# Gated mix of sliding attention and a Mish MLP on one core: another list of steps and other PSUM groups

## The chip, the core and the metric

The kernel runs on one core of a Trainium2 chip. The metric is the time of one execution on the device in microseconds. The core has a matmul engine (TensorE, PE in the profile), a vector engine (VectorE, DVE), a scalar engine (ScalarE, ACT), GpSimd (POOL) and SyncE (SP), which here does little but issue DMAs. Each engine runs its own instructions strictly in the order in which they were written for it, and waits on semaphores for the others.

## What is computed

With x of 2048 rows by 640 columns, all in fp32:

```python
x = A_x
g = _sigmoid((x * gate_w).sum(-1, keepdims=True))
a = _A_ref(x, A_wqkv, A_wo)     # 32 heads of 20; each row attends to itself and to the rows 2, 4 .. 14 before it
b = _B_ref(x, B_w1, B_b1, B_w2) # (mish(x @ w1 + b1)) @ w2, with 1728 hidden columns
return g * a + (1 - g) * b
```

Branch a is x @ wqkv, the windowed softmax attention, and a product with wo. Mish is h * tanh(softplus(h)).

## The kernel before

**Products.** TensorE multiplies in a reduced fp32 form, so every operand is kept as a high and a low part in one buffer (`pair`): ACT copies the rounded high part (L448), and VectorE or GpSimd subtract it to get the low part (L451). Each product is then three matmuls, high by high, high by low, low by high (L516, L517, L518), all into the same PSUM bank. To save matmuls, several products use a fast 2x2 block scheme: sums of blocks are formed on VectorE and GpSimd (L1023, L1245), products of the sums are made, and intermediate results are carried from one PSUM bank into another as a seed: ACT copies the bank (L1150) or VectorE adds to it (L832), and the next products accumulate on top.

**Stages.** Up to about 390 us the kernel works on three things interleaved. First the *units*: eight pieces of x @ wqkv (two halves of the rows by four groups of eight heads), each in eight *slots* of 128 rows. A slot is 15 matmuls of 496 columns into one bank, which ACT empties in three or four copies into the buffer `kvq` (L686, L688, L690). When all eight slots of a unit are there, SP copies the rows that neighbouring positions need within `kvq` (the halo copies, kvq from kvq, of 112 and 15 partitions), and VectorE runs the attention of that unit with multiply and reduce instructions of 2560 elements (L573, L576, L619, L623); ACT adds the exponentials (L596, with a table load) and the weighting (L600), and a copy of q (L579). Units 2 and 3 are made together with the fast scheme, in four *pairs* of slots with steps a1 to c3: a1 to a3 and b1, b2 give unit 2, and store two intermediate results in DRAM (`pu`, `pv`). c0 loads them back in one buffer with two DMAs on SP (L877); c1 copies `pu` from it into a bank (L885, ACT), called ga, and puts six matmuls on top; VectorE then makes the seed of a second bank, de, from ga and `pv` (L832); c2 and c3 finish both for unit 3.

Second the *quads*: x @ w1 in two halves of the rows and six blocks of hidden columns. A quad has banks al, be, ga, de and ep, and steps first (makes al, copied to seed be), second (makes ep, copied by ACT to an `hb` buffer, L1150), m1 to m4, l1 and l2 (the rest). Results leave a bank through Mish on ACT (L1156), or through a sum with the ep copy on VectorE (L1168) and then Mish. Each lands in one of eight `hb` buffers, from which SP stores it to DRAM (L481, the targets are `act11`, `act22`, `actt1` and the like). Sums of two results are formed in the same buffers by GpSimd or VectorE. Some of these sums are made by GpSimd's accumulating DMAs (L1533, L934). The last block of hidden columns (`last`, four banks l0 to l3) is done plainly and leaves through L946.

Third, loads and preparations: `x`, `wq`, `wa`, `wc`, `pieces`, `forms`, `sum` steps bring in inputs and form their sums.

Then the product with w2 and the product with wo follow, up to the end at 615 us. They are not part of the list of steps.

**What sets the order.** The text `ORDER` lists the steps, and at the end of the program each is executed:

```python
for token in ORDER.split():
    do(token)
```

A step only registers tasks with a planner (`class Plan`): the engine, an estimated duration, a rank, what must be done before, which buffers are taken and held. The planner then plays the program through with its estimates. Whenever an engine is free in this play, it gets, of the tasks that are ready and whose buffers are free, the one of the lowest rank and, among these, the one that was registered first; GpSimd also goes by how soon TensorE needs the result. The order that comes out is written down for each engine and is fixed on the chip. TensorE's order so follows the list only where banks and operands are there; buffers of one kind are handed out strictly in the order of the list. Another list, or another group for a bank, can therefore change the order on all five engines, also far from the entry that differs.

**PSUM banks.** Six banks are shared in two groups of three, `qb` and `sb`. A step that needs a bank names it and takes the next free one of a group; the dictionary `BANKS` overrides the group that the code gives:

```python
def bank_buf(name, ring):

    return sb_buf() if BANKS.get(name, ring) == "s" else qb_buf()
```

The name is made of the step: `u65` is unit 6 slot 5, `q12de` is bank de of quad 2 in the second half of the rows, `p22ga` is bank ga of pair 2 of units 2 and 3, `l2` a bank of the last block. A step that takes a bank waits until whoever held that bank before has been read out, and TensorE waits with it.

Of the kernel before, what the change touches and what calls it, by code (L numbers as in the profile page):

```python
# [254 lines left out]
ORDER = """
u.0.5 u.0.6 u.0.4 u.0.7 q.0.0.first last.0 wq.1 q.0.0.m1 q.0.0.m4 q.0.0.m2 sum q.0.0.second q.0.0.m3 pieces.0.1 u.1.0 last.1 u.1.2 q.0.0.l2
q.0.1.first u.1.3 q.0.0.l1 u.1.6 q.0.1.m1 q.0.1.m2 pieces.0.2 q.0.1.m4 u.1.1 q.0.1.second q.0.1.l2 sum q.0.2.first u.1.7 u.1.4 q.0.1.m3 q.0.2.m1
q.0.1.l1 u.1.5 wa.2 q.0.2.second pieces.0.3 pieces.0.4 q.0.2.m3 p.2.0.a1 q.0.2.m4 x.3.1 q.0.2.m2 q.0.2.l2 p.2.2.a1 p.2.1.a1 x.2.4 p.2.0.a2 p.2.1.a2
p.2.0.a3 q.0.2.l1 p.2.2.a2 p.2.3.a1 p.2.3.a2 x.3.3 q.0.3.first p.2.0.b2 p.2.3.a3 p.2.2.a3 p.2.0.c0 p.2.1.a3 p.2.2.b1 q.0.3.m1 p.2.0.b1 x.2.1
q.0.3.second q.0.3.m4 p.2.1.b1 p.2.2.b2 pieces.0.5 p.2.1.c0 q.0.3.m3 x.2.2 wc.2 q.0.4.first q.0.3.m2 q.0.3.l2 q.0.5.first q.0.3.l1 p.2.3.b1 q.0.4.m1  # L260
p.2.2.c0 q.0.4.second q.0.4.m2 q.0.4.m4 p.2.1.b2 p.2.3.c0 p.2.3.b2 q.0.4.m3 wq.4 q.0.4.l1 q.0.4.l2 q.0.5.m1 p.2.0.c1 p.2.2.c1 p.2.3.c1 q.0.5.m2
p.2.2.c2 x.2.3 q.0.5.m4 x.2.0 q.0.5.l2 q.0.5.second p.2.3.c2 p.2.0.c3 p.2.2.c3 p.2.3.c3 p.2.1.c1 p.2.1.c3 p.2.1.c2 x.3.2 third x.3.0 x.3.4 q.0.5.m3
p.2.0.c2 u.4.3 q.0.5.l1 u.4.1 u.4.5 rest.0 u.4.2 sum pieces.1.0 forms.1.0 u.4.7 u.4.6 q.1.0.first u.4.0 q.1.0.m1 wq.5 u.5.4 rest.1 pieces.1.1 u.5.2
u.4.4 q.1.1.first q.1.0.second sum q.1.0.m4 u.5.1 q.1.0.m3 u.5.3 sum q.1.1.second q.1.1.m2 sum u.5.6 q.1.1.m1 pieces.1.2 u.5.0 u.5.7 q.1.1.m4 wq.6
q.1.0.m2 u.5.5 q.1.2.first sum q.1.0.l2 u.6.2 u.6.4 q.1.1.l2 q.1.0.l1 q.1.2.m1 q.1.1.m3 u.6.3 wq.7 u.6.1 q.1.1.l1 u.6.5 u.6.0 u.7.2 u.6.7 u.7.3 u.7.6
q.1.2.second q.1.2.m4 sum pieces.1.3 pieces.1.4 u.6.6 sum q.1.2.m2 q.1.4.first q.1.2.m3 q.1.2.l2 u.7.5 u.7.1 q.1.3.first q.1.3.m2 u.7.4 u.7.0
q.1.3.second pieces.1.5 q.1.2.l1 q.1.3.m1 u.7.7 q.1.4.m1 q.1.4.m4 q.1.4.m2 q.1.3.m4 q.1.3.m3 q.1.3.l2 q.1.4.second q.1.3.l1 q.1.4.l2 rest.2
q.1.5.first q.1.4.m3 q.1.5.m1 q.1.4.l1 q.1.5.m4 q.1.5.m2 lastw.1 q.1.5.second q.1.5.m3 q.1.5.l1 q.1.5.l2 last.2 last.3 rest.3
"""


# [1697 lines left out]
```

## Time and profile before

| what | value |
|---|---|
| median of 3 runs | 616.08 us (615.9 to 616.94) |
| the profiled execution, its own time | 616.89 us |
| its span | 615.1 us |
| TensorE busy | 608.4 us, 99%, 2698 matmuls |
| VectorE busy | 580.3 us, 94% |
| ACT busy | 386.4 us, 63% |
| GpSimd busy | 352.4 us, 57% |
| moved by DMA | 147.01 MB, mean 239 GB/s |

The span lies within the execution; 1.8 us lie around it. The row of a timeline gives the start in us, the duration in us, the engine, the line, the operation and its buffers, and in brackets the idle time ahead of it and what ended it. A row of the stretches gives the bounds, the length, and the busy time and count of TensorE, weight loads, VectorE, ACT and GpSimd, then the granted clock, the share of the DMA engines and GB/s. A row of a DMA view gives the queue, the count, the size and the median time in us from issue to landing. In the group of a line, the numbers behind the bar are total busy us and mean ns of one instruction.

### The profile page before, as it was taken

The page shows a single profiled execution, that of the slowest core. Times are in us where ns is not written, and L with a number is a line of the kernel's source. Part 1 is how long each engine was busy: PE and PEld are TensorE (multiplying, and loading weights), DVE is VectorE, ACT ScalarE, POOL GpSimd, SP SyncE. Part 2 cuts the span into 40 slices and gives each one's busy share as a digit, 9 for nine tenths or more (in the row PEclk, how much of TensorE's full clock was granted, in tenths as well). Part 3 has the DMA queues.
Part 4 walks back from the last instruction along what each step waited for, and adds up shares of the span by engine and source line. Part 5 has one row for each costly group of instructions (what it writes and reads, how often), then busy time and mean ns, then how long its engine had stood idle before and what let it go on. Part 6 is the DMA issues. An engine that isn't in the chain of part 4 may idle for free.

```text
span 615.1 us, 9163 instructions
## 1 busy us (share of the span) xinstructions
PE 608.4 (99%) x2698; PEld 504.7 (82%) x2698; DVE 580.3 (94%) x517; ACT 386.4 (63%) x886; POOL 352.4 (57%) x334
## 2 busy tenths in 40 slices
PE   9999999999999999999999999999999999999997
PEld 6888888887878888888888887888888888888886
DVE  8899999999899999999999999999999999989955
ACT  7687747666786486745746775776857543736520
POOL 1676868967687786376564577775467963001000
PEclk9999999999999999999999999999999999999999
DMA  9774876668696867999984699998989874989913
GB/s 324 233 237 130 274 257 178 237 191 280 214 323 216 270 202 208 266 272 327 242 227 158 179 326 290 278 264 251 268 275 281 248 204 133 286 253 303 278 58 119
DMA packets 101347, 147.01 MB, mean 239 GB/s; under 512 B 11617, under 2 KB 54625, under 8 KB 101073
## 3 DMA queue, kind: packets, MB, share of 16 engines
q1 hardware_dynamic: 97936, 140.66, 70.9%
q0 software_dynamic: 3072, 5.51, 6.5%
q8 instruction: 21, 0.34, 0.2%
q10 hardware_dynamic: 288, 0.26, 0.1%
q14 instruction: 30, 0.24, 0.1%
HBM read 92.38 MB, written 53.03 MB: 236 GB/s over the span
## 4 chain that ended last, share of the span: by engine, by line
PE 93%; DMA 3%; DVE 1%; POOL 1%; issue 1%; ACT 0%; SPq 0%; DVEq 0%; POOLq 0%; ACTq 0%
PE qb L516 15%; PE qb L518 15%; PE qb L517 15%; PE sb L516 15%; PE sb L518 15%; PE sb L517 15%; DMA raw<-in_wq 1%; DMA pair<-pu 1%; DMA actt<-hb 1%; PE qb L680 1%; DVE pr L573 0%; POOL pair L451 0%; DVE lg L576 0%; POOL raw L1023 0%; PE sb L523 0%
## 5 line engine op out<-in xcount | busy, mean ns | idle before, releaser
L451 POOL TENSOR_TENSOR pair<-raw,pair 128x512 fp32r<-128x512 f32 (+3 forms) x142 | 178.0, 1282 | 84.5 <-ACT pair L448 48.2
L448 ACT ACTIVATE pair<-raw 128x512 fp32r<-128x512 f32 (+3 forms) x235 | 136.1, 611 | 49.6 <-PE sb L518 15.8
L516 PE MATMUL qb<-pair 128*128 128x512 f32 (+1 forms) x387 | 150.1, 388 | 2.0 <-ACT qb L885 1.3
L518 PE MATMUL qb<-pair 128*128 128x512 f32 (+1 forms) x387 | 150.0, 388 | 0.0
L517 PE MATMUL qb<-pair 128*128 128x512 f32 (+1 forms) x387 | 149.9, 387 | 0.0
L516 PE MATMUL sb<-pair 128*128 128x512 f32 (+2 forms) x384 | 148.4, 386 | 0.1
L518 PE MATMUL sb<-pair 128*128 128x512 f32 (+2 forms) x384 | 148.2, 386 | 0.0
L517 PE MATMUL sb<-pair 128*128 128x512 f32 (+2 forms) x384 | 148.2, 386 | 0.0
L573 DVE TENSOR_TENSOR pr<-kvq,qg 128x2560 f32<-128x2560 f32 x32 | 90.0, 2811 | 2.6 <-ACT qg L579 1.4
L619 DVE TENSOR_TENSOR pr<-kvq,pg 128x2560 f32<-128x2560 f32 x32 | 90.2, 2820 | 1.0
L576 DVE TENSOR_REDUCE lg<-pr 128x128 f32<-128x2560 f32 x32 | 90.1, 2816 | 0.7
L623 DVE TENSOR_REDUCE kvq<-pr 128x320 f32<-128x2560 f32 x32 | 90.1, 2815 | 0.6
L516 PEld LDWEIGHTS qb<-pair 128*128 128x128 f32 x387 | 72.6, 188 | 17.1 <-ACT qb L885 1.7
L518 PEld LDWEIGHTS qb<-pair 128*128 128x128 f32 x387 | 72.6, 188 | 14.5
L517 PEld LDWEIGHTS qb<-pair 128*128 128x128 f32 x387 | 72.6, 188 | 14.4
L516 PEld LDWEIGHTS sb<-pair 128*128 128x128 f32 x384 | 72.1, 188 | 14.9 <-DVE sb L832 0.5
L517 PEld LDWEIGHTS sb<-pair 128*128 128x128 f32 x384 | 72.1, 188 | 14.2
L518 PEld LDWEIGHTS sb<-pair 128*128 128x128 f32 x384 | 72.1, 188 | 14.2
L451 DVE TENSOR_TENSOR pair<-raw,pair 128x512 fp32r<-128x512 f32 (+2 forms) x93 | 63.6, 705 | 2.8 <-ACT pair L448 2.4
L1023 POOL TENSOR_TENSOR raw<-raw 128x128 f32<-128x128 f32 (+3 forms) x58 | 45.4, 796 | 24.2 <-DMA raw<-in_w 11.6
L1023 POOL TENSOR_TENSOR hb<-hb 128x512 f32<-128x512 f32 x39 | 50.3, 1299 | 9.0 <-DVE lg L595 2.6
L448 ACT ACTIVATE pair<-hb 128x512 fp32r<-128x512 f32 (+3 forms) x62 | 36.5, 589 | 3.9 <-PE qb L518 2.4
(168 smaller groups left out, 745.9 us busy)
## 6 DMA issues: line engine op xcount, KB each, us to landing
actt<-hb SPq DMA_DIRECT2D x52, 256.0 KB, 3.6
raw<-in_w SPq DMA_DIRECT2D x40, 256.0 KB, 3.5
act<-hb SPq DMA_DIRECT2D x38, 256.0 KB, 4.1
raw<-actt SPq DMA_DIRECT2D x37, 256.0 KB, 3.1
raw<-in_wq SPq DMA_DIRECT2D x36, 248.0 KB, 4.1
raw<-act SPq DMA_DIRECT2D x29, 256.0 KB, 3.6
raw<-in_x SPq DMA_DIRECT2D x27, 256.0 KB, 3.7
o<-ot SPq DMA_DIRECT2D x64, 80.0 KB, 3.2
```

The costliest lines, as they stand in the source:

```text
L448: a = add("ACT", act_ns(n), lambda: A.activation(hi(), raw(), AF.Copy), after, rank=rank, take=take, hold=hold)
L451: return (V if e == "DVE" else G).tensor_tensor(lo(), raw(), hi().bitcast(F32), op=OP.subtract)
L516: nc.tensor.matmul(ps, ah, bh, start=first, stop=False, skip_group_check=more)
L517: nc.tensor.matmul(ps, ah, bl, start=False, stop=False, skip_group_check=more)
L518: nc.tensor.matmul(ps, al, bh, start=False, stop=last, skip_group_check=more)
L573: return V.tensor_tensor(pr, window(kv, s0, 0), qg[:, :, None, :].to_broadcast([128, 2, W, QF]), op=OP.mult)
L576: V.tensor_reduce(lg_w[:, s0:s0 + 2], pr.rearrange("p s w (h d) -> p s w h d", d=DH), op=OP.add, axis=AX.X)
L619: V.tensor_tensor(pairs.rearrange("p s k i (h d) -> p s k i h d", d=DH), vw, pg[:, s0:s0 + 2].rearrange("p s (k i) h -> p s k i h", i=2)[: ...
L623: V.tensor_reduce(q[:, s0:s0 + 2], pairs.rearrange("p s k i f -> p s f k i"), op=OP.add, axis=AX.XY)
L680: nc.tensor.matmul(ps.t[:, :n], X[0, kc].t[:, a, i * 128:(i + 1) * 128], WQ[0, kc].t[:, b, :n], start=a == b and kc == 0, stop=False)
L1023: return (V if e == "DVE" else G).tensor_tensor(t.t[:, i:i + n], a.t[:, j:j + n], b.t[:, k:k + n], op=op)
```

## The change

Only `ORDER` and `BANKS` differ. The steps listed are the same ones, each as often as before, and so are the operations (the rows between the `...` of the two lists are of the same kind); their order in the list, the group of many banks, and with these the instruction orders of all five engines differ.

```diff
--- before.py
+++ after.py
@@ -251,21 +251,21 @@
...
-BANKS = {'l0': 's', 'p20al': 's', 'p20de': 's', 'p20ga': 'q', 'p21de': 's', 'p22ga': 'q', 'p23ga': 'q', 'q00al': 's', 'q00be': 'q', 'q00ga': 'q', 'q02al': 's', 'q02de': 'q', 'q03be': 'q', 'q03de': 'q', 'q03ep': 's', 'q03ga': 'q', 'q04al': 's', 'q05be': 'q', 'q05ep': 's', 'q10de': 'q', 'q11al': 's', 'q11de': 'q', 'q11ga': 'q', 'q12al': 's', 'q12de': 'q', 'q13be': 'q', 'q13ga': 'q', 'q14al': 's', 'q14de': 'q', 'q14ep': 's', 'q14ga': 'q', 'q15al': 's', 'q15de': 'q', 'q15ga': 'q', 'u04': 's', 'u06': 's', 'u11': 's', 'u12': 's', 'u13': 's', 'u16': 's', 'u17': 's', 'u42': 's', 'u43': 's', 'u46': 's', 'u52': 's', 'u53': 's', 'u54': 's', 'u57': 's', 'u64': 's', 'u65': 's', 'u72': 's', 'u73': 's', 'u74': 's', 'u75': 's', 'u76': 's'}
+BANKS = {'l0': 's', 'l1': 's', 'l2': 's', 'l3': 's', 'p20al': 's', 'p20de': 's', 'p20ep': 's', 'p20ga': 'q', 'p21de': 's', 'p22ep': 's', 'p22ga': 'q', 'p23ga': 'q', 'q00ga': 'q', 'q01de': 'q', 'q01ep': 's', 'q02de': 'q', 'q02ga': 'q', 'q03ep': 's', 'q04al': 's', 'q05be': 'q', 'q05ep': 's', 'q10de': 'q', 'q12al': 's', 'q12de': 'q', 'q12ga': 'q', 'q13be': 'q', 'q13ep': 's', 'q13ga': 'q', 'q14al': 's', 'q14de': 'q', 'q14ep': 's', 'q14ga': 'q', 'q15al': 's', 'q15be': 'q', 'q15de': 'q', 'q15ep': 's', 'q15ga': 'q', 'u05': 's', 'u10': 's', 'u15': 's', 'u17': 's', 'u41': 's', 'u43': 's', 'u44': 's', 'u45': 's', 'u51': 's', 'u52': 's', 'u54': 's', 'u56': 's', 'u61': 's', 'u63': 's', 'u70': 's', 'u71': 's', 'u72': 's', 'u73': 's', 'u75': 's', 'u76': 's', 'u77': 's'}
 ORDER = """
...
-p.2.2.c0 q.0.4.second q.0.4.m2 q.0.4.m4 p.2.1.b2 p.2.3.c0 p.2.3.b2 q.0.4.m3 wq.4 q.0.4.l1 q.0.4.l2 q.0.5.m1 p.2.0.c1 p.2.2.c1 p.2.3.c1 q.0.5.m2
-p.2.2.c2 x.2.3 q.0.5.m4 x.2.0 q.0.5.l2 q.0.5.second p.2.3.c2 p.2.0.c3 p.2.2.c3 p.2.3.c3 p.2.1.c1 p.2.1.c3 p.2.1.c2 x.3.2 third x.3.0 x.3.4 q.0.5.m3
-p.2.0.c2 u.4.3 q.0.5.l1 u.4.1 u.4.5 rest.0 u.4.2 sum pieces.1.0 forms.1.0 u.4.7 u.4.6 q.1.0.first u.4.0 q.1.0.m1 wq.5 u.5.4 rest.1 pieces.1.1 u.5.2
...
-q.1.0.m2 u.5.5 q.1.2.first sum q.1.0.l2 u.6.2 u.6.4 q.1.1.l2 q.1.0.l1 q.1.2.m1 q.1.1.m3 u.6.3 wq.7 u.6.1 q.1.1.l1 u.6.5 u.6.0 u.7.2 u.6.7 u.7.3 u.7.6
-q.1.2.second q.1.2.m4 sum pieces.1.3 pieces.1.4 u.6.6 sum q.1.2.m2 q.1.4.first q.1.2.m3 q.1.2.l2 u.7.5 u.7.1 q.1.3.first q.1.3.m2 u.7.4 u.7.0
...
-q.1.5.first q.1.4.m3 q.1.5.m1 q.1.4.l1 q.1.5.m4 q.1.5.m2 lastw.1 q.1.5.second q.1.5.m3 q.1.5.l1 q.1.5.l2 last.2 last.3 rest.3
...
+q.0.5.m1 p.2.3.b1 q.0.4.m3 q.0.4.m4 x.2.1 p.2.0.c1 p.2.0.c3 p.2.2.b2 x.3.4 q.0.4.l1 p.2.3.c0 p.2.2.c1 q.0.4.l2 p.2.3.c1 q.0.5.m2 q.0.5.m4 q.0.5.l2
+p.2.2.c2 p.2.1.b2 p.2.2.c3 q.0.5.second p.2.0.c2 p.2.1.c1 p.2.3.c3 x.2.2 x.3.0 p.2.3.c2 p.2.1.c2 x.2.0 wq.4 p.2.1.c3 third u.4.5 q.0.5.m3 rest.0
...
+q.1.1.second u.5.7 u.6.1 u.5.5 u.6.6 u.6.0 q.1.1.m3 wq.7 u.6.3 u.7.6 q.1.1.l2 q.1.2.m1 u.6.7 q.1.2.second u.6.5 pieces.1.3 q.1.2.m2 u.7.3 sum u.7.0
+q.1.2.m4 pieces.1.4 u.7.1 q.1.2.m3 q.1.1.l1 u.6.4 u.6.2 q.1.3.first q.1.2.l2 q.1.3.m1 u.7.2 q.1.3.second q.1.2.l1 q.1.4.first u.7.4 pieces.1.5 sum
+q.1.3.m4 q.1.3.m3 q.1.3.l1 q.1.4.m2 q.1.4.m1 q.1.3.m2 u.7.7 u.7.5 q.1.4.m4 q.1.3.l2 q.1.4.second q.1.5.first q.1.4.m3 q.1.5.m1 q.1.4.l1 lastw.1
+q.1.5.m4 q.1.4.l2 q.1.5.second q.1.5.m2 q.1.5.m3 q.1.5.l1 q.1.5.l2 last.2 last.3 rest.2 rest.3
...
```

Three places show what that does to the queues. In the rows, `qb`, `sb`, `hb`, `pair` and `raw` are followed by a running number that tells one use of a buffer from another; "out <- in" as in the profile.

ACT around the first c1 steps of the tail of units 2 and 3 (176 us in the profile); `pair_1972`, `pair_1823` and `pair_1782` are the buffers loaded by c0. Before:

```order
L1156 ACT_TABLE_LOAD
L1156 ACTIVATE hb_2037<-qb_1765,bias_75 128x512
L885 ACTIVATE qb_2040<-pair_1972 128x496
L1156 ACTIVATE hb_2048<-sb_2001,bias_75 128x512
L1150 ACTIVATE hb_2058<-sb_2028 128x512
L885 ACTIVATE sb_2061<-pair_1823 128x496
```

And now:

```order
L1156 ACT_TABLE_LOAD
L1156 ACTIVATE hb_2037<-qb_1734,bias_75 128x512
L885 ACTIVATE qb_2040<-pair_1782 128x496
L1156 ACTIVATE hb_2047<-sb_1995,bias_75 128x512
L1150 ACTIVATE hb_2058<-sb_2029 128x512
L885 ACTIVATE sb_2061<-pair_1972 128x496
```

The first of the two seeds reads another buffer. In SP's queue the load of `pair_1972` stands at the same row before and now, and that of `pair_1782` 25 rows ahead of it; these rows are from SP's queue now:

```order
L877 DMA pair_1782<-pu2_2_260 128x496
L877 DMA pair_1782<-pv2_2_256 128x496
...
L481 DMA raw_1952<-in_wq 128x512
L481 DMA act21_0_4_101<-hb_1941 128x512
L481 DMA o1_189<-ot_1904 32x5x128
L481 DMA raw_1969<-in_wq 128x512
L877 DMA pair_1972<-pu2_1_259 128x496
L877 DMA pair_1972<-pv2_1_255 128x496
```

ACT around the copy of quad 15's ep (374 us in the profile), which frees that bank; the last row reads the bank l2 of the last block. Before:

```order
L1156 ACT_TABLE_LOAD
L1156 ACTIVATE hb_3996<-sb_3796,bias_75 128x512
L1150 ACTIVATE hb_3998<-qb_3921 128x512
L448 ACTIVATE pair_4024<-raw_3880 128x512
L1156 ACTIVATE hb_4028<-qb_3909,bias_75 128x512
...
L946 ACTIVATE hb_4076<-qb_4006,bias_75 128x512
```

And now:

```order
L1150 ACTIVATE hb_3966<-sb_3892 128x512
...
L448 ACTIVATE pair_3993<-raw_3873 128x512
L1156 ACT_TABLE_LOAD
L1156 ACTIVATE hb_3997<-sb_3821,bias_75 128x512
L448 ACTIVATE pair_4021<-raw_3878 128x512
L1156 ACTIVATE hb_4025<-qb_3922,bias_75 128x512
...
L946 ACTIVATE hb_4071<-sb_4000,bias_75 128x512
```

The copy (the L1150 row) moved from behind the table load and one Mish to six rows ahead of the table load, and ep and l2 are now in the sb group.

ACT and SP near 302 us, in the order now. `qb_3213` is the bank of unit 6 slot 5, `qb_3229` that of quad 12's de, `qb_3274` that of unit 6 slot 4; unit 6 slot 2 takes the bank of `qb_3229` next. `hb_3304` takes the buffer of `hb_3242`. ACT:

```order
L448 ACTIVATE pair_3234<-raw_3172 128x496
L1156 ACTIVATE hb_3240<-hb_3240,bias_75 128x512
L686 ACTIVATE kvq1_269<-qb_3213 128x320
L688 ACTIVATE kvq1_269<-qb_3213 128x160
L690 ACTIVATE hx_81<-qb_3213 128x16
L448 ACTIVATE pair_3268<-raw_3204 128x496
L579 ACTIVATE qg_273<-kvq0_268 128x320
L1156 ACTIVATE hb_3304<-qb_3229,bias_75 128x512
L686 ACTIVATE kvq1_269<-qb_3274 128x320
```

SP:

```order
L481 DMA raw_3244<-in_w1 128x512
L481 DMA raw_3260<-in_w1 128x512
L481 DMA raw_3264<-in_w1 128x128
L481 DMA kvq1_269<-kvq1_269 112x960
L481 DMA kvq1_269<-kvq1_269 15x960
L481 DMA actt1_1_1_133<-hb_3242 128x512
L481 DMA actt3_1_1_161<-hb_2886 128x512
```

Before, the store to `actt1_1_1_133` stands 19 rows behind the last halo copy in SP's queue; the rows around it there are:

```order
L481 DMA raw_3129<-in_wo 128x2x256
L481 DMA raw_3131<-in_wo 128x2x256
L481 DMA act22_1_1_119<-hb_2761 128x512
L481 DMA actt1_1_1_133<-hb_3123 128x512
L481 DMA actt3_1_1_161<-hb_3096 128x512
```

Now the store follows the two halo copies directly, and these wait for the L686 row of `qb_3213`.

More of the change, by code (lines that the diff above doesn't have):

```diff
@@ L255 @@
 ORDER = """
[L256 to L259, printed above, removed]
@@ L260 @@
-q.0.3.second q.0.3.m4 p.2.1.b1 p.2.2.b2 pieces.0.5 p.2.1.c0 q.0.3.m3 x.2.2 wc.2 q.0.4.first q.0.3.m2 q.0.3.l2 q.0.5.first q.0.3.l1 p.2.3.b1 q.0.4.m1
-p.2.2.c0 q.0.4.second q.0.4.m2 q.0.4.m4 p.2.1.b2 p.2.3.c0 p.2.3.b2 q.0.4.m3 wq.4 q.0.4.l1 q.0.4.l2 q.0.5.m1 p.2.0.c1 p.2.2.c1 p.2.3.c1 q.0.5.m2
-p.2.2.c2 x.2.3 q.0.5.m4 x.2.0 q.0.5.l2 q.0.5.second p.2.3.c2 p.2.0.c3 p.2.2.c3 p.2.3.c3 p.2.1.c1 p.2.1.c3 p.2.1.c2 x.3.2 third x.3.0 x.3.4 q.0.5.m3
-p.2.0.c2 u.4.3 q.0.5.l1 u.4.1 u.4.5 rest.0 u.4.2 sum pieces.1.0 forms.1.0 u.4.7 u.4.6 q.1.0.first u.4.0 q.1.0.m1 wq.5 u.5.4 rest.1 pieces.1.1 u.5.2
@@ L264 @@
-u.4.4 q.1.1.first q.1.0.second sum q.1.0.m4 u.5.1 q.1.0.m3 u.5.3 sum q.1.1.second q.1.1.m2 sum u.5.6 q.1.1.m1 pieces.1.2 u.5.0 u.5.7 q.1.1.m4 wq.6
-q.1.0.m2 u.5.5 q.1.2.first sum q.1.0.l2 u.6.2 u.6.4 q.1.1.l2 q.1.0.l1 q.1.2.m1 q.1.1.m3 u.6.3 wq.7 u.6.1 q.1.1.l1 u.6.5 u.6.0 u.7.2 u.6.7 u.7.3 u.7.6
-q.1.2.second q.1.2.m4 sum pieces.1.3 pieces.1.4 u.6.6 sum q.1.2.m2 q.1.4.first q.1.2.m3 q.1.2.l2 u.7.5 u.7.1 q.1.3.first q.1.3.m2 u.7.4 u.7.0
-q.1.3.second pieces.1.5 q.1.2.l1 q.1.3.m1 u.7.7 q.1.4.m1 q.1.4.m4 q.1.4.m2 q.1.3.m4 q.1.3.m3 q.1.3.l2 q.1.4.second q.1.3.l1 q.1.4.l2 rest.2
@@ L268 @@
-q.1.5.first q.1.4.m3 q.1.5.m1 q.1.4.l1 q.1.5.m4 q.1.5.m2 lastw.1 q.1.5.second q.1.5.m3 q.1.5.l1 q.1.5.l2 last.2 last.3 rest.3
+u.0.5 u.0.7 u.0.4 wq.1 u.0.6 q.0.0.first q.0.0.second q.0.0.m1 last.0 q.0.0.m4 q.0.0.l2 q.0.0.m3 pieces.0.1 q.0.1.first u.1.7 u.1.2 q.0.1.m1 q.0.0.l1
+q.0.1.second sum q.0.0.m2 sum q.0.1.m3 q.0.1.m4 u.1.4 pieces.0.2 u.1.3 last.1 u.1.1 q.0.1.l1 q.0.1.m2 u.1.0 q.0.1.l2 u.1.5 q.0.2.first u.1.6 wa.2
+q.0.2.m1 q.0.2.m2 q.0.2.second p.2.2.a1 p.2.1.a1 q.0.2.m4 p.2.0.a1 q.0.2.m3 p.2.0.a2 q.0.2.l1 p.2.1.a2 pieces.0.3 p.2.0.a3 q.0.2.l2 p.2.3.a1 x.2.3
@@ new lines @@
+p.2.1.a3 pieces.0.4 p.2.0.b2 p.2.1.b1 p.2.2.a2 x.2.4 x.3.2 p.2.0.b1 p.2.3.a2 p.2.3.a3 pieces.0.5 q.0.3.first q.0.3.m1 x.3.1 p.2.2.a3 p.2.2.c0 p.2.3.b2
+q.0.3.second q.0.3.m3 q.0.3.m4 q.0.3.l1 q.0.4.first q.0.4.m1 q.0.3.l2 q.0.3.m2 p.2.0.c0 q.0.4.m2 q.0.5.first x.3.3 p.2.2.b1 q.0.4.second wc.2 p.2.1.c0
+q.0.5.m1 p.2.3.b1 q.0.4.m3 q.0.4.m4 x.2.1 p.2.0.c1 p.2.0.c3 p.2.2.b2 x.3.4 q.0.4.l1 p.2.3.c0 p.2.2.c1 q.0.4.l2 p.2.3.c1 q.0.5.m2 q.0.5.m4 q.0.5.l2
+p.2.2.c2 p.2.1.b2 p.2.2.c3 q.0.5.second p.2.0.c2 p.2.1.c1 p.2.3.c3 x.2.2 x.3.0 p.2.3.c2 p.2.1.c2 x.2.0 wq.4 p.2.1.c3 third u.4.5 q.0.5.m3 rest.0
@@ new lines @@
+q.0.5.l1 pieces.1.0 sum u.4.6 u.4.7 u.4.2 forms.1.0 q.1.0.first u.4.4 u.4.0 u.4.3 wq.5 sum pieces.1.1 u.4.1 q.1.0.second q.1.0.m1 rest.1 u.5.6 u.5.2
+q.1.0.m4 u.5.3 pieces.1.2 u.5.1 q.1.1.first u.5.4 wq.6 q.1.1.m1 sum q.1.0.m3 q.1.1.m4 q.1.1.m2 sum q.1.2.first q.1.0.l2 sum q.1.0.l1 u.5.0 q.1.0.m2
+q.1.1.second u.5.7 u.6.1 u.5.5 u.6.6 u.6.0 q.1.1.m3 wq.7 u.6.3 u.7.6 q.1.1.l2 q.1.2.m1 u.6.7 q.1.2.second u.6.5 pieces.1.3 q.1.2.m2 u.7.3 sum u.7.0
+q.1.2.m4 pieces.1.4 u.7.1 q.1.2.m3 q.1.1.l1 u.6.4 u.6.2 q.1.3.first q.1.2.l2 q.1.3.m1 u.7.2 q.1.3.second q.1.2.l1 q.1.4.first u.7.4 pieces.1.5 sum
```

## The prediction

> **What bounds the kernel now.** I read the page first: part 1 for the busy shares, part 2 for the slices, part 4 for the chain that ended last.
>
> ```profile
> span 615.1 us, 9163 instructions
> PE 608.4 (99%) x2698; PEld 504.7 (82%) x2698; DVE 580.3 (94%) x517; ACT 386.4 (63%) x886; POOL 352.4 (57%) x334
> PEclk9999999999999999999999999999999999999999
> PE 93%; DMA 3%; DVE 1%; POOL 1%; issue 1%; ACT 0%; SPq 0%; DVEq 0%; POOLq 0%; ACTq 0%
> ```
>
> TensorE is busy 99% of the span, at the full granted clock in every slice, and 93% of the last chain is matmuls. The change keeps all 2698 of them, so their own time is fixed. All that a new order can win is the time in which TensorE stands still between matmuls; all that it can lose is new time of that kind. So next comes the question where TensorE stands still: the busy time in stretches of 15 us, then the rows in the stretches that are not full.
>
> ```profile
> 135.00:150.00 15.00, 14.87 (x66) 11.99 (x65) 14.66 (x9) 10.97 (x22) 10.88 (x9) 1.00 0.82 257
> 165.00:180.00 15.00, 13.64 (x59) 10.48 (x58) 14.31 (x11) 12.92 (x28) 12.01 (x11) 1.00 0.88 257
> 360.00:375.00 15.00, 14.27 (x63) 11.52 (x62) 13.49 (x14) 12.90 (x25) 12.20 (x10) 1.00 0.93 307
> 180.00:360.00 180.00, 180.00 (x808) 151.27 (x807) 176.59 (x119) 115.03 (x307) 116.04 (x122) 1.00 0.80 239
> ```
>
> The second number is TensorE's busy time. Between the start-up and 600 us only three stretches are short of their 15.00; from 180 to 360 us, for one, nothing is missing, and its 808 matmuls give the usual pace: 180 / 808 = 0.223 us from start to start, a mean of the forms of 512 columns (0.227) and 496 columns (0.220). The rows of TensorE's timeline around each stall:
>
> ```profile
> 146.64 0.39 PE L518 MATMUL qb<-kvq,pair 128*128 128x512 f32 x1
> 147.16 0.50 PE L516 MATMUL qb<-kvq,pair 128*128 128x512 f32 x1
> 147.50 0.40 PE L517 MATMUL qb<-kvq,pair 128*128 128x512 f32 x1
> ...
> 168.13 0.39 PE L518 MATMUL qb<-pair 128*128 128x512 f32 x1
> 168.63 0.49 PE L516 MATMUL sb<-pair 128*128 128x496 f32 x1
> ...
> 175.30 0.39 PE L518 MATMUL sb<-pair 128*128 128x512 f32 x1
> 176.94 0.49 PE L516 MATMUL qb<-pair 128*128 128x496 f32 x1 [1.25 <-ACT qb L885]
> ...
> 178.16 0.39 PE L518 MATMUL qb<-pair 128*128 128x496 f32 x1
> 178.51 0.49 PE L516 MATMUL sb<-pair 128*128 128x496 f32 x1
> ...
> 372.87 0.39 PE L518 MATMUL qb<-pair 128*128 128x512 f32 x1
> 373.99 0.50 PE L516 MATMUL qb<-pair 128*128 128x512 f32 x1 [0.73 <-ACT hb L1150]
> 374.32 0.39 PE L517 MATMUL qb<-pair 128*128 128x512 f32 x1
> ```
>
> The loss of a stall is the gap between the starts less the usual 0.23 or 0.22, and the first matmul behind it costs another 0.11 (its successor starts 0.33 or 0.34 later, see the rows at 147.50 and 374.32). So the stall at 147 us costs (0.52 - 0.23) + 0.11 = 0.40; the one at 168.6 us (0.50 - 0.23) + 0.11 = 0.38; the one at 177 us (1.64 - 0.23) + 0.11 = 1.52, with 0.13 + 0.11 = 0.24 more at 178.5 us, together 1.76; the one at 374 us (1.12 - 0.23) + 0.10 = 0.99. Sum 3.53 us. That is the most this order can give: with no stall left, the median 616.08 becomes 612.55.
>
> **The change part by part.** It adds and removes no instruction. For each stall I ask what TensorE waited for, and whether that comes sooner in the new order.
>
> At 177 us the first matmul of c1 (unit 2, pair 2) waits for its PSUM seed, and the seed for a transfer:
>
> ```profile
> 176.30 0.59 ACT L885 ACTIVATE qb<-pair 128x496 f32<-128x496 f32 x1 [1.89 <-DMA pair<-pu]
> 170.19 1.08 SPq L877 DMA_DIRECT2D pair<-pu  x1
> pair<-pu SPq DMA_DIRECT2D x1, 248.0 KB, 6.0
> ```
>
> The load was issued at 170.19 and took 6.0 us to land. In the new order the same place reads a pair whose load stands 25 rows earlier in SP's queue (rows 153 and 178), so it is long there: 1.52 us gone. The pair in row 178 is now read by the c1 behind it, six matmuls later (6 x 0.22 = 1.3 us). Without the stall the first c1 starts at 176.94 - 1.41 = 175.53, the second at about 176.9 at the earliest; its seed can end at 176.2 + 0.6 = 176.8 if the load is issued and lands as before. ACT's mish and a seed copy ahead of it are done by then. That is level; I take the 0.24 at 178.5 us as gone too, and carry 0.3 us for this place among the small waits below.
>
> At 374 us the last block's second output takes the qb bank of quad 15's ep, freed by a copy that stands in ACT's queue behind a table load and a mish:
>
> ```profile
> 371.47 1.28 ACT L1156 ACT_TABLE_LOAD   x1
> 372.76 0.69 ACT L1156 ACTIVATE hb<-sb,bias 128x512 f32<-128x512 f32 x1
> 373.35 0.59 ACT L1150 ACTIVATE hb<-qb 128x512 f32<-128x512 f32 x1
> ```
>
> In the new order this copy stands ahead of the table load (six rows before it), and the last block uses banks of the sb group. 0.99 us gone. At 147 us the bank of quad 05's al was freed by a mish behind others in ACT's queue; that step now comes earlier, with a bank that was freed before. 0.40 us gone. At 168.6 us the de of pair 0 waits for a late sum of VectorE, and stands at the same place of TensorE's new order: I leave that 0.38 in. So 1.52 + 0.24 + 0.99 + 0.40 = 3.15 us are taken off.
>
> Now what is late next. Going through the new order for banks that are retaken soon after their reader, one place stands out, near 302 us. Slot 2 of unit 6 takes the qb bank of quad 12's de. That bank is freed by a mish on ACT, which needs an hb buffer, which is free only when a store of the earlier hb lands; and SP issues that store right behind the two halo copies of kvq, which wait for ACT to empty the bank of unit 6's slot 5. I run a clock from the last matmul of slot 5. TensorE needs the bank after 12 matmuls of de, 15 of slot 4 and 9 of ga: 21 x 0.227 + 15 x 0.220 = 8.07 us. On the other side:
>
> ```profile
> 301.39 0.72 ACT L1156 ACTIVATE hb<-hb,bias 128x512 f32<-128x512 f32 x1 [0.61 <-DVE hb L1168]
> 304.66 0.41 ACT L686 ACTIVATE kvq<-qb 128x320 f32<-128x320 f32 x1
> 305.26 2.47 SPq L481 DMA_DIRECT2D kvq<-kvq  x2
> 82.57 0.73 ACT L1156 ACTIVATE hb<-hb,bias 128x512 f32<-128x512 f32 x1 [2.98 <-DMA act<-hb]
> ```
>
> ACT is free for the evacuation after at most one mish (0.72), and needs 0.41: 1.1 us, or 1.7 with a wait for VectorE as the 0.61 in the row. The two halo issues take up to 2.5 us; I take 1.5, since the second need not wait. The mish at the end takes 0.7, with 0.05 until TensorE goes on. The store must then land within 8.07 - (1.1 to 1.7) - 1.5 - 0.75 = 4.1 to 4.7 us. How long such a transfer takes:
>
> ```profile
> actt<-hb SPq DMA_DIRECT2D x52, 256.0 KB, 3.6
> actt<-hb SPq DMA_DIRECT2D x1, 256.0 KB, 2.0
> actt<-hb SPq DMA_DIRECT2D x1, 256.0 KB, 4.2
> ot<-o SPq DMA_DIRECT2D x1, 256.0 KB, 5.6
> ot<-o SPq DMA_DIRECT2D x1, 256.0 KB, 6.2
> ```
>
> The median of all 52 such stores is 3.6 us, the fastest (57.5 us) 2.0; one directly behind a halo copy (85 us) took 4.2; two transfers behind a halo with an accumulating DMA of GpSimd in flight (270 and 293.5 us) took 6.2 and 5.6. In the new order three loads, the halo and such a GpSimd DMA stand just ahead of the store, so the last two rows are nearest: 5.9 us, against an allowance of 4.4, is a stall of 1.5, and 0.1 for the restart: 1.6 us. Bounds: 0 (any of the first three rows), and 2.1 + 0.1 = 2.2 (6.2 against 4.1). The mish row at 82.57 us is the same wait in the old order, 2.98 us for the store of its hb; there TensorE did not stop, because no bank hung on it.
>
> [...]
>
> Last, small waits. An order planned this tight has places where a bank or a seed comes just in time; before, two of them missed by 0.40 and 0.38. One is kept already, 0.3 is the c1 above, and I add 0.3 for one more: 0.6 us, bounds 0 and 1.5 (four such misses).
>
> The sum against the median: 616.08 - 3.15 + 1.6 + 0.6 = **615.1 us**. Against the profiled execution's own 616.89 it is 615.94; that execution lies 0.81 above the median, and I keep to the median. Below 0.2% (1.23 us) a measurement of this kernel can't tell a difference from none; 615.1 is 0.95 us or 0.16% below: **no change that can be told, on the faster side**. Its own range is 614.2 to 616.6.
>
> **The rivals.**
>
> Faster: the store near 302 us lands within its allowance. The 52 stores' median of 3.6 speaks for it, the 5.6 and 6.2 behind halo and GpSimd against it. Then 615.1 - 1.6 = 613.5, and 612.55 with no small waits and the 168.6 us place clear.
>
> Slower: VectorE is one instruction late near 295 us. ACT's mish ahead of the evacuation waits for VectorE's sum L1168, and VectorE's queue holds the long attention products just ahead of it:
>
> ```profile
> L573 DVE TENSOR_TENSOR pr<-kvq,qg 128x2560 f32<-128x2560 f32 x32 | 90.0, 2811 | 2.6 <-ACT qg L579 1.4
> ```
>
> One such instruction is 2.8 us. If VectorE lags by one, evacuation, halos, store, mish and bank all move by 2.8: the stall is 1.6 + 2.8 = 4.4 us and the time 615.1 + 2.8 = 617.9. It decides from a lag of 2.2 us on (617.31, the point from which slower can be told). For it speaks that VectorE is busy 176.59 of the 180 us up to 360, so a lag isn't made up; against it that before ACT's longest wait of this kind there was 0.61. [...]
>
> Not as it says: the stall at 177 us only moves to the second c1, because the load in SP's row 178 again lands late, 1 us later than before, and near 302 us the 1.6 comes on top. Then 615.1 + 1.4 = 616.5. This is still no change.
>
> **How the numbers follow.** The main case has 0.36, the faster rival 0.33, the slower one 0.17, the moved stall 0.10; 0.04 is for gains between the cases. Of the main case a little lies under 614.85. So faster 0.38, no change 0.45, slower 0.17. The range runs from 612.7, just above the floor of 612.55, to 617.7, which leaves out most of the slower rival and little else.
>
> **What would show it.** Right: the profile of the changed kernel has TensorE's stretch from 360 to 375 us full; the seed before the first c1 near 175.5 us waits for no transfer; a stall of 1 to 2 us near 302 us, put down to ACT's L1156 on hb, and that mish itself to a DMA from hb. Wrong: no pause there (faster rival); a pause above 3 us with ACT waiting for VectorE's L1168 before it (slower rival); a pause over 1 us at a seed L885 near 177 us (moved stall); or a pause over 1 us at any place not named here, which I can't see from the order and which would make the sum wrong altogether.

## The result, and where the time went

The changed kernel takes 620.15 us (median of 9 runs, 617.22 to 621.91) against 616.24 us before (9 runs, 614.72 to 617.59). The ratio is 1.0057, with a 95% interval from 1.0041 to 1.0073, which is some 3.5 us (the medians lie 3.9 us apart): slower, clear of the 0.2% and outside the predicted range. The profiled execution took 620.64 us, with a span of 618.9 against 615.1.

The page after, parts 1 and 2:

```profile
span 618.9 us, 9169 instructions
PE 611.4 (99%) x2698; PEld 506.5 (82%) x2698; DVE 578.9 (94%) x518; ACT 387.5 (63%) x886; POOL 352.6 (57%) x333
PEclk9999999999999999999899999999999999999999
```

The busy shares in part 1 hardly differ from before. The granted clock differs in one digit: it is 8 in the slice from 294 to 309 us. The stretches of the kernel after (bounds, length, busy time and count of TensorE, weight loads, VectorE, ACT and GpSimd, then granted clock, DMA share and GB/s) show the rest:

```profile
135.00:150.00 15.00, 15.00 (x68) 12.45 (x67) 14.86 (x11) 10.66 (x23) 11.37 (x9) 1.00 0.88 254
165.00:180.00 15.00, 15.00 (x68) 12.36 (x67) 14.38 (x13) 13.84 (x32) 12.49 (x11) 1.00 1.01 321
300.00:315.00 15.00, 12.25 (x43) 9.79 (x42) 13.70 (x11) 8.40 (x21) 9.12 (x10) 0.77 0.89 236
305.00:310.00 5.00, 3.74 (x9) 3.08 (x10) 3.77 (x5) 4.03 (x12) 2.14 (x3) 0.55 0.98 327
310.00:315.00 5.00, 5.00 (x19) 4.08 (x19) 4.93 (x4) 4.38 (x9) 5.00 (x5) 0.77 0.72 151
360.00:375.00 15.00, 15.00 (x68) 12.43 (x67) 14.80 (x11) 11.84 (x26) 10.40 (x10) 1.00 0.91 299
```

The three stretches that were short before are full now. In their place the one from 300 to 315 us has 43 matmuls at a granted clock of 0.77. Before, it had 70:

```profile
300.00:315.00 15.00, 15.00 (x70) 12.72 (x69) 14.86 (x11) 10.29 (x30) 12.41 (x17) 1.00 0.90 224
```

From 310 to 315 us TensorE is "busy" all 5.00 us, but with 19 matmuls rather than the 25 of before: busy time alone doesn't show a slow clock, the count and the clock do. TensorE's timeline after, around the pause:

```profile
303.13 0.39 PE L518 MATMUL qb<-pair 128*128 128x512 f32 x1
306.26 0.78 PE L516 MATMUL qb<-pair 128*128 128x496 f32 x1 [2.75 <-ACT hb L1156]
306.84 0.61 PE L517 MATMUL qb<-pair 128*128 128x496 f32 x1
...
312.21 0.43 PE L518 MATMUL qb<-pair 128*128 128x496 f32 x1
312.48 0.39 PE L516 MATMUL sb<-pair 128*128 128x496 f32 x1
```

The pause costs 306.26 - 303.13 - 0.23 = 2.90 us. The 15 matmuls behind it take 312.48 - 306.26 = 6.22 us, some 0.41 us each, where 15 x 0.22 = 3.30 is usual: 2.92 us more. So one place costs 5.8 us, and half of it is not the wait but the clock behind it.

The account of the two spans: 3.53 us of old stalls are gone; 2.90 and 2.92 are new here; small stalls at 50 us (0.29), 65 us (0.16) and 177 us (0.15) cost 0.60; the start-up takes 0.39 more (the 101st matmul starts at 25.66 us rather than 25.27; in another execution of the same kernel it is 25.14, so this is scatter and not the change). That gives +3.3 of the +3.8 us; the other 0.5 is spread too thin for me to place.

### The profile page after: what moved, and what is told of

It is laid out like the page before. It is cut to its first block, busy times and chain, and to the rows that moved or that the text cites. A ratio compares the mean times of both kernels' runs of the same rounds, so it can differ in the third digit from the quotient of the medians.

```text
span 618.9 us, 9169 instructions
## 1 busy us (share of the span) xinstructions
PE 611.4 (99%) x2698; PEld 506.5 (82%) x2698; DVE 578.9 (94%) x518; ACT 387.5 (63%) x886; POOL 352.6 (57%) x333
## 4 chain that ended last, share of the span: by engine, by line
PE 95%; DMA 2%; ACT 1%; DVE 1%; issue 0%; SPq 0%; DVEq 0%; ACTq 0%
PE sb L516 16%; PE sb L517 16%; PE sb L518 16%; PE qb L516 15%; PE qb L517 15%; PE qb L518 15%; DMA hb<-in_x 1%; DMA kvq<-kvq 1%; DMA raw<-in_wq 1%; DVE pr L619 0%; PE qb L680 0%; ACT pair L448 0%; SPq L481 0%; PE sb L522 0%; PE qb L523 0%
## 5 line engine op out<-in xcount | busy, mean ns | idle before, releaser
L451 POOL TENSOR_TENSOR pair<-raw,pair 128x512 fp32r<-128x512 f32 (+3 forms) x136 | 170.0, 1273 | 75.9 <-ACT pair L448 60.1
L448 ACT ACTIVATE pair<-raw 128x512 fp32r<-128x512 f32 (+3 forms) x235 | 137.7, 613 | 48.8 <-DMA raw<-actt 12.8
L516 PE MATMUL sb<-pair 128*128 128x512 f32 (+2 forms) x421 | 162.7, 386 | 0.0
L517 PE MATMUL sb<-pair 128*128 128x512 f32 (+2 forms) x421 | 162.6, 386 | 0.0
L518 PE MATMUL sb<-pair 128*128 128x512 f32 (+2 forms) x421 | 162.5, 386 | 0.0
L516 PE MATMUL qb<-pair 128*128 128x512 f32 (+1 forms) x350 | 137.0, 391 | 2.7 <-ACT hb L1156 2.7
L517 PE MATMUL qb<-pair 128*128 128x512 f32 (+1 forms) x350 | 136.8, 391 | 0.0
L518 PE MATMUL qb<-pair 128*128 128x512 f32 (+1 forms) x350 | 136.6, 390 | 0.0
L516 PEld LDWEIGHTS sb<-pair 128*128 128x128 f32 x421 | 79.1, 188 | 16.1 <-ACT sb L885 0.3
L518 PEld LDWEIGHTS sb<-pair 128*128 128x128 f32 x421 | 79.0, 188 | 15.6
L517 PEld LDWEIGHTS sb<-pair 128*128 128x128 f32 x421 | 79.1, 188 | 15.5
L619 DVE TENSOR_TENSOR pr<-kvq,pg 128x2560 f32<-128x2560 f32 x32 | 90.3, 2820 | 1.0
L516 PEld LDWEIGHTS qb<-pair 128*128 128x128 f32 x350 | 66.4, 190 | 16.6 <-ACT hb L1156 3.2
L518 PEld LDWEIGHTS qb<-pair 128*128 128x128 f32 x350 | 66.4, 190 | 13.4
L517 PEld LDWEIGHTS qb<-pair 128*128 128x128 f32 x350 | 66.4, 190 | 13.2
L451 DVE TENSOR_TENSOR pair<-raw,pair 128x512 fp32r<-128x512 f32 (+3 forms) x99 | 69.4, 722 | 5.7 <-ACT pair L448 5.5
L1023 POOL TENSOR_TENSOR hb<-hb 128x512 f32<-128x512 f32 x42 | 55.2, 1331 | 11.6 <-DVE pg L609 4.0
L1023 POOL TENSOR_TENSOR raw<-raw 128x128 f32<-128x128 f32 (+3 forms) x53 | 42.5, 818 | 21.9 <-DVE raw L1023 8.4
L451 POOL TENSOR_TENSOR pair<-hb,pair 128x512 fp32r<-128x512 f32 (+2 forms) x29 | 35.0, 1211 | 15.7 <-ACT pair L448 8.1
```

Source lines behind the costliest of these rows:

```text
L448: a = add("ACT", act_ns(n), lambda: A.activation(hi(), raw(), AF.Copy), after, rank=rank, take=take, hold=hold)
L451: return (V if e == "DVE" else G).tensor_tensor(lo(), raw(), hi().bitcast(F32), op=OP.subtract)
L516: nc.tensor.matmul(ps, ah, bh, start=first, stop=False, skip_group_check=more)
L517: nc.tensor.matmul(ps, ah, bl, start=False, stop=False, skip_group_check=more)
L518: nc.tensor.matmul(ps, al, bh, start=False, stop=last, skip_group_check=more)
L619: V.tensor_tensor(pairs.rearrange("p s k i (h d) -> p s k i h d", d=DH), vw, pg[:, s0:s0 + 2].rearrange("p s (k i) h -> p s k i h", i=2)[: ...
```

## The experiments

Three theories and a question. **Pause and clock**: the store of one hb buffer lands late, TensorE stops for 2.9 us, and the stop itself lowers the clock. **Rival A**: the clock falls by itself in this order. **Rival B**: the store is late because the DMA engines are full, wherever it stands in its queue. The question within the first: what makes that store's landing so long: the halo copies ahead of it, or GpSimd's accumulating DMA.

For the edits a few tasks got a name, and a task can be held back: the planner plays as before, but the held instruction is written out only behind another one that is named. So all other rows of all five engines stay in place.

```diff
+HOLD, held = {}, []
+def emit(t, e):
+    ins = held.append((HOLD[t.tag], t.fn)) if t.tag in HOLD else t.fn(e) if t.both else t.fn()
+    return [x[1]() for x in held if x[0] == t.tag and t.tag] and None or ins
...
-                    ins = t.fn(e) if t.both else t.fn()
+                    ins = emit(t, e)
...
```

**The store three rows sooner.** One load and the two halo copies are held until the store.

```diff
-HOLD, held = {}, []
+HOLD, held = {x: ("put", "t1", 1, 1) for x in (("dc", 3), ("halo", 6, 0, 0), ("halo", 6, 0, 1))}, []
```

> The changed kernel with one edit on SyncE's queue: near 297 us the store of the hb buffer is issued ahead of one small load and of the two halo copies, three rows sooner. Theory (the pause of 2.9 us near 303 us comes from the late store, and the half clock behind it from the pause): the store is issued 1.5 to 2 us sooner, the pause shrinks to about 1 us, the granted clock is 1.000 and the time falls by 1.8 + 3.0 to about 615.3 us. Rival A (the clock falls by itself in this order, not through the pause): the time falls by 1.8 us only, to 618.3, with the clock still 0.994 to 0.997. Rival B (the store is late because the DMA engines are full, wherever it stands): the pause stays at 2.9 us and the time at 620.

Measured: 614.30 us (10 runs, 613.59 to 615.91) against 616.91 before on the same chip (25 runs); ratio 0.9956, interval 0.9936 to 0.9976. Its stretch from 300 us, and then, of its timeline, the store's issue and the mish that waits for the landing:

```profile
300.00:315.00 15.00, 15.00 (x70) 12.74 (x69) 14.90 (x11) 9.52 (x27) 10.96 (x13) 1.00 0.91 251
```

```profile
295.56 0.33 SPq L481 DMA_DIRECT2D actt<-hb  x1
...
299.07 0.69 ACT L1156 ACTIVATE hb<-qb,bias 128x512 f32<-128x512 f32 x1 [1.11 <-DMA actt<-hb]
```

The store was issued at 295.56 and the mish that waits for it began at 299.07: 3.5 us. No pause is left and the clock is 1.00. Rivals A and B both fall. The gain was larger than expected, since the landing shrank too. This kernel is 2.6 us faster than the one before and 5.1 to 5.9 us faster than the one after (619.39 and 620.15), from three rows of SP's queue.

**Useless work in the pause.** Zero weights times ones, added to the bank ga ahead of its last product, so that TensorE is busy through part of the wait. This computes nothing; the sum it adds to is unchanged.

```diff
+                    [nc.tensor.matmul(ps.t, zeros, ones[:, :], start=False, stop=False, skip_group_check=True) for _ in range(fill if k == len(todo) - 1 else 0)]; ...
...
-            t = self.mms(self.ga, self.plain(1, 1), [self.sd])
+            t = self.mms(self.ga, self.plain(1, 1), [self.sd], fill=12 if (self.P, self.q) == (1, 2) else 0)
...
```

> The changed kernel with 12 matmuls of a zero weight added to the bank ga just before the pause near 303 us, so that TensorE works through nearly all of the wait; nothing waits for them that is not late anyway. The wait itself is not shortened. Theory (the pause drops the clock): clock 1.000 in every run, time 620.15 - 3.0 = 617.2 us, though TensorE has 2.7 us more work. Rival A (the clock falls by itself): clock 0.994 to 0.997 as before, time 620.2.

> As the run with 12, with 4 such matmuls: TensorE still idles some 1.9 us of the 2.75. Theory: if a pause of 1.9 us is short enough to keep the clock, 617.2 us and 1.000; if not, 619 to 620 and 0.994 to 0.997. Before, 1.25 us did not lower it. Rival A: 620.2 and 0.994 to 0.997.

With 12: 617.88 us (10 runs; ratio to before 1.0019, interval 1.0000 to 1.0038), the clock 0.999 or 1.000 in every run. Six of the ten took 617.27 to 617.97 us and four 619.29 to 619.95, so a step of some 2 us also comes without the clock, and these runs don't show from what. With 4: 617.65 us (10 runs; 1.0016, 0.9996 to 1.0036); the clock 0.997 in two runs (619.29 and 620.07 us) and 0.999 or 1.000 in eight (seven of these 616.99 to 617.76, one 619.81). TensorE's timeline with 12, and then the stretch behind:

```profile
302.15 2.78 PE L1131 MATMUL qb<-const-bfloat16-1.0,gap 128*128 128x512 bf16 x12
...
305.92 0.49 PE L516 MATMUL qb<-pair 128*128 128x496 f32 x1 [0.28 <-ACT hb L1156]
306.25 0.38 PE L517 MATMUL qb<-pair 128*128 128x496 f32 x1
```

```profile
305.00:310.00 5.00, 4.72 (x21) 3.67 (x20) 4.35 (x5) 4.81 (x14) 2.48 (x3) 1.00 0.96 326
```

The useful matmul still starts near 306 us: the wait is as long as in the kernel after. But TensorE idles 0.28 us rather than 2.75, and the clock stays 1.00. Twelve useless matmuls take 1.5 to 2.3 us off the median (617.88 against 619.39 and 620.15). The clock's share, apart from the wait's, is of that size: 1.6 to 2.9 us in the traces. With 4, the profiled run was one of the two with the clock at 0.997:

```profile
306.01 0.49 PE L516 MATMUL qb<-pair 128*128 128x496 f32 x1 [1.82 <-ACT hb L1156]
...
306.67 0.61 PE L518 MATMUL qb<-pair 128*128 128x496 f32 x1
...
309.92 0.39 PE L517 MATMUL qb<-pair 128*128 128x496 f32 x1
```

So the clock fell behind an idle time of 1.82 us, but in only two of ten runs by the mean clock.

**Pauses in the kernel before.** The first matmul of 13 slots also waits for the VectorE instruction that is running when it is written out (0), or for the next one (1).

```diff
+PAUSE, late, dve = {'u14': 0, 'u17': 1, 'u41': 1, 'u47': 0, 'u52': 1, 'u53': 0, 'u56': 1, 'u64': 0, 'u61': 1, 'u66': 0, 'u72': 0, 'u75': 1, 'u73': 0}, [], []
+def emit(t, e, follow):
+    ins = late.append(t) if PAUSE.get(t.tag) == 1 else t.fn(e) if t.both else t.fn(); e == "DVE" and ins and dve.append(ins); PAUSE.get(t.tag) == 0 and follow(ins, dve[-1])
+    return [follow(late.pop().fn(), ins) for _ in range(len(late) if e == "DVE" and ins else 0)] and None or ins
...
```

> The kernel before, with 13 pauses put in: the first matmul of 13 slots of the units also waits for the instruction that VectorE is just in, or for its next one. Pauses of some tenths of a us up to about 4 us, in an order that has none there. Theory: behind each long pause (above some 2 us) the matmuls start 0.41 us apart for one or two windows of 3 to 4 us; behind short ones (below 1.3 us) they keep 0.22. Rival A: the clock stays 1.00 behind all of them.

One run: 625.83 us (616.91 before); it is read only for the clock behind the pauses. Most pauses were shorter than meant. TensorE's longest waits in it (what waited for what: us in total, times, longest), and then its stretches around two of them:

```profile
PE qb L516 <- DVE ot L529: 3.6, 2, 3.2
PE sb L516 <- DVE hb L1023: 1.0, 1, 1.0
PE sb L516 <- DVE sm L607: 0.9, 1, 0.9
```

```profile
192.00:195.50 3.50, 0.48 (x3) 0.06 (x1) 3.47 (x3) 2.88 (x8) 2.97 (x3) 1.00 0.91 293
195.50:196.57 1.07, 0.93 (x4) 0.82 (x5) 1.07 (x3) 1.00 (x4) 0.36 (x1) 1.00 1.07 319
196.58:199.99 3.41, 3.41 (x10) 2.65 (x9) 3.24 (x4) 0.50 (x1) 0.78 (x2) 0.50 1.01 360
200.00:204.00 4.00, 4.00 (x19) 3.26 (x19) 3.88 (x3) 1.13 (x5) 1.77 (x4) 1.00 0.59 172
236.40:240.00 3.60, 3.55 (x16) 3.02 (x17) 3.43 (x3) 1.88 (x2) 1.40 (x3) 1.00 0.99 216
```

Behind the pause of 3.2 us, and there alone, the clock falls, though not at once: it is 1.00 for the first matmuls behind the pause, 0.50 from 196.58 to 199.99 us, and 1.00 from then on. Behind the one of 0.9 us (236.4 us) it is 1.00. So a pause of 3.16 us lowered the clock to 0.50 in the kernel before, too, at a place that has nothing of the change's order.

**What made the landing long.** In one run GpSimd's accumulating DMA is held behind GpSimd's next sum, in another only the halo copies are held behind the store, in a third GpSimd's DMA goes ahead by two rows while the halo copies stay behind.

```diff
+HOLD, held = {("ot2", 0, 1): ("a4", 1, 1)}, []
+HOLD, held = {x: ("put", "t1", 1, 1) for x in (("halo", 6, 0, 0), ("halo", 6, 0, 1))}, []
+HOLD, held = {("halo", 6, 0, 0): ("put", "t1", 1, 1), ("halo", 6, 0, 1): ("put", "t1", 1, 1), ("a1", 1, 1): ("ot2", 0, 1), ("a3", 1, 1): ("ot2", 0, 1)}, []
```

> The changed kernel with GpSimd's accumulating DMA (issued at 297.8 us, 1.1 us before the store, 7.4 us to landing) put behind GpSimd's next sum, some 3 us later. The store stays behind the two halo copies. If that DMA makes the store's landing long: 6.5 us falls to about 4.2 us as behind a halo alone, the pause near 303 us from 2.75 to 0.5 us, the clock stays 1.000. If the halo copies ahead make it long: still 6 to 6.5 us, a pause over 2 us, and a lowered clock in most runs.

> The changed kernel with the store only ahead of the two halo copies, but behind all three loads; GpSimd's DMA stays. The store is issued at about 297.4 instead of 298.9 us. If the halo copies ahead make the landing long: about 3.5 us as in the first experiment, landed at 301, no pause. If GpSimd's DMA 0.4 us behind it does, or the full engines: 6 us or more, landed at 303.5, a pause of about 1 us.

> The store ahead of the two halo copies, as in the run before, but GpSimd's accumulating DMA put two GpSimd rows earlier, so that it is issued about 2 us ahead of the store. If such a DMA in flight alone makes the store long: 6 to 7 us from its issue (near 297.5) to landing, 304, and a pause of some 1 us. If it takes the halo copies and that DMA together: about 4 us, no pause, 614.4 us with clock 1.000.

> The changed kernel itself, again, on the chip of these runs: 619 to 621 us with clock 0.994 to 0.997 in most runs, 617 to 618 in those at 1.000; about 5 us more than the first experiment's 614.3.

> The kernel in which only GpSimd's DMA is one row later, timed: 614.4 us as in its one look, 2.4 us below the kernel before, if no other pause opens; the clock 1.000. By rival A, 618.

The kernel after, again: 619.39 us (6 runs, 618.17 to 620.74; ratio 1.0048, 1.0028 to 1.0068), the clock 0.994 to 0.997 in all six. The single runs: 614.42 us with GpSimd's DMA later, 614.46 with the halo copies behind, 615.25 with GpSimd's DMA ahead and the halo copies behind; the clock 0.999 or 1.000. The first of them timed: 614.31 us (6 runs; ratio 0.9965, 0.9942 to 0.9987).

From the timelines, by time: the store's issue (with the stores right behind it where they are one group), GpSimd's DMA and the mish that waits for the landing. First with GpSimd's DMA one row later:

```profile
298.26 1.60 SPq L481 DMA_DIRECT2D actt<-hb  x3
...
300.89 0.82 POOL L1533 DMA_DIRECT2D ot<-ot  x1
...
301.98 0.69 ACT L1156 ACTIVATE hb<-qb,bias 128x512 f32<-128x512 f32 x1 [3.17 <-DMA actt<-hb]
```

With the halo copies behind the store:

```profile
296.72 0.38 SPq L481 DMA_DIRECT2D actt<-hb  x1
...
297.68 0.81 POOL L1533 DMA_DIRECT2D ot<-ot  x1
...
300.79 0.69 ACT L1156 ACTIVATE hb<-qb,bias 128x512 f32<-128x512 f32 x1 [2.00 <-DMA actt<-hb]
```

With GpSimd's DMA ahead and the halo copies behind:

```profile
296.38 0.81 POOL L1533 DMA_DIRECT2D ot<-ot  x1 [3.34 <-DVE hb L1168]
...
298.54 0.33 SPq L481 DMA_DIRECT2D actt<-hb  x1
...
302.85 0.69 ACT L1156 ACTIVATE hb<-qb,bias 128x512 f32<-128x512 f32 x1 [3.55 <-DMA actt<-hb]
```

And in the kernel after, again, issued at 297.88 behind the halo copies and GpSimd's DMA (297.26):

```profile
305.30 0.69 ACT L1156 ACTIVATE hb<-qb,bias 128x512 f32<-128x512 f32 x1 [6.95 <-DMA actt<-hb]
```

From issue to the mish that waits:

| ahead of the store | us |
|---|---|
| halo copies and GpSimd's DMA (after; after again; with 12 and with 4 useless matmuls) | 6.6; 7.4; 6.5; 7.1 |
| halo copies alone (and the same, timed) | 3.7; 3.9 |
| GpSimd's DMA alone | 4.3 |
| neither; GpSimd's DMA 1.0 us behind | 4.1 |
| neither; GpSimd's DMA 1.3 us behind | 3.5 |

Each alone costs under a microsecond; both together cost 2.4 us or more (6.5 against 4.1). My expectations set the one against the other, and neither was right by itself: taking away either one is enough. With GpSimd's DMA ahead and the halo copies behind, the pause of 0.4 us comes from the later issue, since GpSimd's sum that the store needs was itself later. That row is one execution, and its DMA stood 2.2 us ahead of the store, against 0.6 to 1.1 us in the kernel after. Why the two together hold a store up is not shown by these runs.

## Why the prediction was wrong, point by point

**The gains were right.** All four stalls are gone: 3.53 us where 3.15 were taken off. That the one at 168.6 us went too was not foreseen, and why it went stays open. At 177 us the reasoning held. From the timeline after:

```profile
174.84 0.58 ACT L885 ACTIVATE qb<-pair 128x496 f32<-128x496 f32 x1
...
176.39 0.60 ACT L885 ACTIVATE sb<-pair 128x496 f32<-128x496 f32 x1
...
176.78 0.39 PE L518 MATMUL qb<-pair 128*128 128x496 f32 x1
177.04 0.49 PE L516 MATMUL sb<-pair 128*128 128x496 f32 x1
```

The first seed waits for no transfer. The second ends at 176.99 us, where 176.8 was reckoned, and its c1 starts 0.04 us late, which with the 0.11 behind it costs 0.15. That disposes of the moved stall. The small waits, put at 0.6 us, were 0.60, but that is luck: 0.45 of it stands at 50 and 65 us, which the prediction didn't name.

**The place of the loss was right, its price was the mis-sized term.** The pause near 302 us came where the prediction put it, on ACT's mish and the store before it. I gave 1.6 us with 2.2 as the upper bound; it was 2.90, and 3.35 in the other profile. The timeline after, and then the store's landing (queue, count, size, us from issue to landing):

```profile
295.24 2.05 SPq L481 DMA_DIRECT2D raw<-in_w  x3
295.77 0.72 ACT L1156 ACTIVATE hb<-hb,bias 128x512 f32<-128x512 f32 x1 [1.56 <-DVE hb L1168]
296.40 0.42 ACT L686 ACTIVATE kvq<-qb 128x320 f32<-128x320 f32 x1
...
297.38 1.46 SPq L481 DMA_DIRECT2D kvq<-kvq  x2
297.83 0.81 POOL L1533 DMA_DIRECT2D ot<-ot  x1
...
298.93 2.22 SPq L481 DMA_DIRECT2D actt<-hb  x3
...
305.52 0.69 ACT L1156 ACTIVATE hb<-qb,bias 128x512 f32<-128x512 f32 x1 [6.58 <-DVE pr L619]
```

```profile
actt<-hb SPq DMA_DIRECT2D x1, 256.0 KB, 6.5
```

By the prediction's own clock, which starts where slot 5's last matmul is through (295.29): the evacuation was done at 296.82, so 1.53 us, within the 1.1 to 1.7. But SP was still issuing three loads until 297.29, a wait of about half a microsecond that the sum did not have. The halos took 1.46, as taken. The landing took 6.5 to 6.6, above the 5.9 taken and the bound of 6.2. Half a microsecond and 0.7 are most of the 1.3 us that were missing. In the other profile, where the pause was 3.35, SP was through with its loads at 296.25 us, as the evacuation ended (296.23), and the landing alone took 1.5 us more than was taken (7.4). A trap in reading: the profile here puts the mish's wait down to VectorE's L619. The other profile of the same kernel names the store, and moving the store moved the mish. The slower rival was wrong in its mechanism: VectorE did make ACT wait longer (1.56), but that was not what decided.

**The step that failed is the one that took a pause to cost what it lasts.** The sum and its range had no fall of the clock, because a pause of 1.25 us had left it at 1.00 before. Behind the pause of 2.75 us it fell to 0.50. Without the fall, the account is 616.08 - 3.53 + 0.60 + 2.90 + 0.11 = 616.16, and no change would have been right. The fall adds 2.9 us where the clock stayed low for 6.83 us, as in the profiled run (616.16 - 0.11 + 2.92 = 618.97, outside the range, though still 1.2 us below the median of 620.15), and 1.6 to 1.7 us where it stayed low for 3.41 us. In the 15 runs of the kernel after, the mean clock was 1.000 in one (617.22 us), 0.996 or 0.997 in nine (618.17 to 620.74) and 0.994 in five (620.43 to 621.91). The kernels that have the wait and mostly keep the clock took 617.88 and 617.65; with the 616.91 that the kernel before took beside them the account without the fall gives 616.99, so 0.7 to 0.9 us stays unexplained there too. The rows of before would have allowed the right step: the longest pause there, 1.25 us, was no bound for a longer one, so the fall of the clock belonged into the range for any pause above it.

The traces show how far it fell, and when. The granted clock stood at 0.50 for 3.41 us (306.43 to 309.84 with 4 useless matmuls, 196.58 to 199.99 in the run with pauses) or for 6.83 us (305.47 to 312.30 in the kernel after), behind pauses of 1.82, 3.16 and 2.75 us. In the clock record of the kernel after, which starts at 5.10 us, it had stood at 1.00 for 300.37 us up to the fall, and it stood there for 307.20 us from the rise on: 88 and 90 times 3.413 us, which is half of the 6.827 us between them. Stretches of 3.41 us around the fall, three of the kernel after and two of the one with 4 useless matmuls:

```profile
302.06:305.47 3.41, 1.45 (x7) 0.87 (x5) 3.41 (x5) 0.00 (x0) 0.00 (x0) 1.00 1.00 303
305.48:308.88 3.40, 2.62 (x6) 2.16 (x7) 2.17 (x5) 3.36 (x11) 1.02 (x1) 0.50 0.96 307
308.89:312.29 3.40, 3.40 (x10) 2.72 (x9) 3.37 (x3) 2.48 (x4) 3.40 (x4) 0.50 0.93 227
...
303.02:306.43 3.41, 1.59 (x8) 0.95 (x6) 2.87 (x2) 1.16 (x5) 0.00 (x0) 1.00 0.99 300
306.44:309.84 3.40, 3.40 (x10) 2.73 (x9) 2.74 (x3) 2.75 (x10) 2.22 (x3) 0.50 0.96 335
```

TensorE had idled 1.96 and 1.82 us of the 3.41 us at whose end the clock fell, and 3.06 and 2.48 us in the other two runs (the kernel after again, and the one with pauses). Behind the pauses of 1.25 us in the kernel before and of 0.9 us in the run with pauses the clock stayed at 1.00. From what idle time on it falls, and why the same wait left a mean clock of 0.994 in some runs of the kernel after, 0.996 or 0.997 in others and 1.000 in one, is not shown by these runs.

**Faster, no change, slower**: the faster rival needed the store in time. That it was within reach is shown by the kernels with one row moved, at 614.3 us.
